# Start-up order and transposes ahead of the values' products in a fused attention and MLP-mixer kernel

## The chip, the cores and the metric

One core of one Trainium2 chip runs the whole program. The metric is device microseconds (us) of one execution, as the median of several runs. The engines have short names below: PE is TensorE (its weight loads are listed as PEld), DVE is VectorE, ACT is ScalarE, POOL is GpSimd, and SP is SyncE, whose queue issues most of the DMAs.

## The reference, cut to what matters

```python
q, k, v: (8, 12, 448, 64) float32      # batch, heads, sequence, head width
def rmsnorm(x, g):
    return x / np.sqrt(np.mean(x * x, axis=-1, keepdims=True) + 1e-06) * g
scores = matmul(rmsnorm(q, g_q), rmsnorm(k, g_k).T) / sqrt(64)
attn = softmax(scores)
x = matmul(attn, v)                     # then (batch, 448, 768), heads side by side
# token and channel mixer; its four weights are float64
u = x + (relu(x.T @ w_tok1) @ w_tok2).T      # 448 -> 256 -> 448
out = u + relu(u @ w_ch1) @ w_ch2            # 768 -> 1536 -> 768
```

## The kernel before, in words

**Work and stages.** The 96 heads are taken as 48 pairs, six pairs for each of the eight batches. The attention of one batch always runs one batch ahead of the mixer of the batch before it. So the program begins with the attention of batch 0 alone ("the first attention"). Beside it, and beside the first mixer, the float64 weights are converted to float32 by bit operations and stored in a form that the later products read back.

**One pair.** `load_qk` (L880) brings queries and keys to SBUF, `squares` (L900) squares them on ACT (L913) into the one buffer `sq` and sums each row on DVE (L917), and `roots` (L926) makes reciprocal roots with ten short DVE operations (L946 to L951). `scale` (L262) multiplies the queries alone by their roots, on POOL (L272). Keys are never scaled: their root goes in as the scale of the exponential on ACT (`exp`, L292). `trans_qk(p, i)` (L274) transposes queries (i = 0) or keys (i = 1) with four PE transposes into a PSUM tile `t_ps` (L282), and ACT brings the tile to the SBUF tile `qkT` with the factor g (L284). `score` (L295) and `score_last` (L308) multiply, and `av` (L397) and `av_last` (L409) form the products with the values; in the first attention each also has a product with a column of ones (L382), which sums the weights. `finish` calls `denominator` (L430), whose four DVE operations begin with the transpose `dt` at L444, which waits for those sums.

**Steps.** `att_step(g)` (L461) is one of four steps s = g mod 4 for two pairs p and p + 1. Each step has `scores()` and then `products()`: s = 0 has the first two score blocks of pair p and the products of the pair before; s = 1 the third block and the first two products; s = 2 the last short blocks of both pairs (L316) and the first block of pair p + 1; s = 3 its two other blocks, then `av_last` of both, a product and `finish(p)`. Behind a step stand items of cost 0: `load_v`; at s = 0 `squares(p + 2)`; at s = 1 `squares(p + 3)`, the roots of both and two `scale`s. At odd s the two `trans_qk` of the next pair come after all these. Below, "step 7" is the step with g = 7.

**Weights.** Chunk i of the weights takes one item, `one(i)` (L230). It issues the load of chunk i + 2, puts bits together for chunk i - 2 on DVE (L209), does the first conversion of chunk i on DVE (L189, L190, L192), the second of chunk i - 1 on ACT (L200, L202), and the last of chunk i - 2 on POOL (L224, and for later weights L163 to L166).

**What sets the order.** The order on PE, DVE, ACT and POOL inside `whole` is that in which the program issues instructions; each engine takes its own strictly in that order. `merge` (L29) mixes the attention's items with the weights' items by their costs. SP's queue is in order too. The four PSUM tiles of `ps_S` are shared by scores and transposes in rotation: a new tile waits until ACT has read the one four tiles earlier. So a pair's `t_ps` at s = 3 takes the tiles of the first score block of the same step, and at s = 1 those of the second block of the step before.

**Start.** The class `Start` runs ahead of the branch on the two gains (`tc.If`). It sets zeros in the five query-and-key buffers on DVE (L850 to L853), loads pairs 0 and 1 (the keys of pair 0 on ACT's queue), makes constants on POOL, and forms squares and roots of pair 0. Then `whole` issues: `load_v(0)`, two weight loads, `scale(0)` on POOL, the change of g at L789, `trans_qk(0, 0)`, `trans_qk(0, 1)`, more loads, and then squares, roots, `swap` and `scale` of pair 1, all ahead of step 0.

Of the kernel before, what the change touches and what calls it, by code (L numbers as in the profile page):

```python
# [46 lines left out]
def whole(ctx, tc, shifted, pre, q, k, v, g_q, g_k, moe_w_tok1, moe_w_tok2, moe_w_ch1, moe_w_ch2, out):  # L47
# [211 lines left out]

        return slice((a ^ p % 2) * D, (a ^ p % 2) * D + D)  # L260

    def scale(p):  # L262

        n = 2 * NS
        qk, rs = st["qk", p], st["rs", p]
        parts = [(R, 0, n, rs[0:R, 0:n].unsqueeze(2))]
        if shifted:
            parts.append((P, n, n - 2, rs[:, n:2 * n - 2].unsqueeze(2)))
            parts.append((P, 2 * n - 2, 2, rs[:, 2 * n - 2:2 * n - 1].unsqueeze(2)))
        for rows, o, m, r in parts:  # L270
            x = qk[0:rows, o * D:(o + m) * D].rearrange("p (r d) -> p r d", d=D)
            nc.gpsimd.tensor_tensor(out=x, in0=x, in1=r.to_broadcast([rows, m, D]), op=ALU.mult)  # L272

    def trans_qk(p, i):  # L274
        qk = st["qk", p]
        if i == 0:
            st["qkT", p] = qkT_pool.tile([P, S + NS * P], F32, name="qkT")
        ps = s_tile("t_ps")
        n = P if i else R
        for c in range(NS):  # L280
            o = (i * NS + c) * P
            nc.tensor.transpose(ps[:, c * n:(c + 1) * n], qk[0:n, o:o + P], ident[0:n, 0:n])  # L282
        to = st["qkT", p][:, S:S + NS * P] if i else st["qkT", p][:, 0:S]
        nc.scalar.mul(to, ps[:, 0:NS * n], g_t[:, i:i + 1])  # L284
        if i == 1:
            st.pop(("qk", p))

    def e_tile():
# [172 lines left out]
    def att_step(g):  # L461


        t, s = divmod(g, 4)
        p = 2 * t
        live = g < NG
        items = []

        def scores():
            if s == 0:  # L470
                score(p, 0)
                score(p, 1)
# [36 lines left out]

        def tiled():  # L510
            if shifted:
                if live:
                    both_shifted()
                return
            if live:
                scores()
            products()

        items.append((3.75 if s in (0, 3) else 2.25, tiled))
        if live and p >= NPAIR and not shifted:  # L520

            parts = {0: [(p, 0)], 1: [(p, 1)], 2: [(p, 2)], 3: [(p + 1, 0), (p + 1, 1), (p + 1, 2)]}[s]
            items += [(0.5, lambda pp=pp, part=part: chunk_sums(pp, part)) for pp, part in parts]
        if live and s % 2 == 1 and p + (s + 1) // 2 < NP:
            items.append((0.0, lambda: load_v(p + (s + 1) // 2)))
        if live and s < 2 and p + 2 + s < NP:
            items.append((0.0, lambda: pre.squares(p + 2 + s, st)))
            if s == 1:
                items.append((0.0, lambda: pre.roots(p + 2, 2, st)))
                items.append((0.0, lambda: swap(p + 3)))  # L530
                items += [(0.0, lambda i=i: scale(p + 2 + i)) for i in range(2)]
        q = p + (s + 1) // 2
        if live and s % 2 == 1 and q < NP:
            items += [(0.4, lambda i=i: trans_qk(q, i)) for i in range(2)]
            if q + 3 < NP:
                items.append((0.0, lambda: pre.load_qk(q + 3, st)))
        return items
# [243 lines left out]
    BEFORE = len(first) + 10  # L781
    then = len(first) + stage_end[4] + 4

    load_v(0)
    weight_load(0)
    weight_load(1)
    scale(0)

    nc.vector.tensor_scalar(g_t[:, 0:1], g_t[:, 0:1], float(D) ** 0.5, None, ALU.mult)  # L789
    trans_qk(0, 0)  # L790
    trans_qk(0, 1)
    pre.load_qk(2, st)
    for i in range(2, 5):
        weight_load(i)
    pre.load_qk(3, st)
    pre.squares(1, st)
    pre.roots(1, 1, st)
    swap(1)
    scale(1)
    per = NPAIR * 2  # L800
    att_items = lambda lo, hi: [it for g in range(lo, hi) for it in att_step(g)]
    for _, fn in merge(att_items(0, AHEAD * per + 1), weight_items(0, BEFORE)):
        fn()
    left = []
    for b in range(B):
# [19 lines left out]
class Start:  # L825


    def __init__(self, ctx, tc, q, k, g_q, g_k, w2):
        self.nc = nc = tc.nc
        self.q, self.k = q, k  # L830
        B, H, S, D = q.shape
        self.NPAIR, self.NS, self.D = H // 2, 4, D
        self.R = S // self.NS
        P = 128
        pool = lambda name, bufs: ctx.enter_context(tc.tile_pool(name=name, bufs=bufs))
        const = pool("start", 1)
        KF = w2.shape[0] // P // 2
        self.hb = const.tile([P, len(HB), KF, S // 2], F32, name="hb")

        n = 2 * self.NS * 2 * D  # L840
        flat = self.hb[:].rearrange("p q f s -> p (q f s)")
        assert flat.shape[-1] >= 2 * n
        self.st = {}
        self.qk_t = [const.tile([P, n], F32, name=f"qk_{i}") for i in range(3)]
        for p in range(2):
            self.st["qk", p] = flat[:, p * n:(p + 1) * n]
        self.v_t = [const.tile([P, (2 * self.NS - 1) * D], F32, name=f"v_{i}") for i in range(2)]

        for qk in [self.st["qk", p] for p in range(2)] + self.qk_t:
            nc.vector.memset(qk[96:P, 0:n // 2], 0.0)  # L850
            o = n - 2 * D
            nc.vector.memset(qk[D:P, o:o + D], 0.0)
            nc.vector.memset(qk[0:D, o + D:o + 2 * D], 0.0)  # L853
        self.load_qk(0, self.st, other=nc.scalar)
        self.load_qk(1, self.st)
        self.g_t = const.tile([P, 2], F32, name="g_t")
        for i, g in enumerate((g_q, g_k)):
            for a in range(2):
                nc.gpsimd.dma_start(
                    out=self.g_t[a * D:(a + 1) * D, i:i + 1], in_=g.rearrange("(p o) -> p o", o=1))  # L860
        self.ident = const.tile([P, P], F32, name="ident")
        make_identity(nc, self.ident[:, :])
        self.one_c = const.tile([P, D], F32, name="one_c")
        nc.gpsimd.memset(self.one_c[:], 1.0)
        self.expo_c = const.tile([P, 1], F32, name="expo_c")
        nc.gpsimd.memset(self.expo_c[:], -896.0 * 2**23)
        self.sq = const.tile([P, 4 * self.NS, D + 1], F32, name="sq")
        nc.gpsimd.memset(self.sq[:, 0:4 * self.NS - 2, D:D + 1], D * 1e-6)
        nc.gpsimd.memset(self.sq[:, 4 * self.NS - 2:4 * self.NS, D:D + 1], D * 0.5e-6)
        self.st["rs", 0] = const.tile([P, 4 * self.NS], F32, name="rs_0")  # L870
        with tc.tile_pool(name="st_0", bufs=1) as self.st_pool:
            self.nt_pool = self.st_pool
            self.squares(0, self.st, halves=((0, 1), (1, 2)))
            self.st.pop(("ms", 0))

    def heads(self, p):
        b, j = divmod(p, self.NPAIR)
# [2 lines left out]
    def load_qk(self, p, st, other=None):  # L880
# [14 lines left out]
                out=k[:, :, a], in_=self.k[b, hs][a][0:nk].rearrange("(p c) d -> p c d", c=NS - 1))  # L895
        for a in range(2):
            o = 4 * NS * D - 2 * D + a * D
            (other or self.nc.sync).dma_start(out=qk[a * D:(a + 1) * D, o:o + D], in_=self.k[b, hs][a][nk:])

    def squares(self, p, st, halves=((0, 2),)):  # L900

# [8 lines left out]
        for lo, hi in halves:  # L910
# [8 lines left out]
            if hi == 2 * n:  # L919

                nc.vector.tensor_tensor(
                    out=ms[:, hi - 2:hi - 1], in0=ms[:, hi - 2:hi - 1], in1=ms[:, hi - 1:hi], op=ALU.add)
            if len(halves) > 1:
# [97 lines left out]
```

## Time and profile before

| | |
|---|---|
| median of 3 runs | 1482.06 us (1481.83 to 1483.47) |
| the profiled execution, whole | 1482.08 us |
| its span, first to last instruction | 1480.3 us |
| PE busy | 1394.3 us (94%), 7048 matmuls |
| DVE busy | 718.4 us (49%) |
| ACT busy | 470.7 us (32%) |
| POOL busy | 475.4 us (32%) |
| first matmul of the scores | starts at 16.49 us |
| last `dt` of the first attention (pair 5) | starts at 100.67 us |

The span runs from the first instruction to the last; 1.8 us of the execution lie around it. In the profile's rows, a number in brackets such as [1.53 <-ACT qkT L284] is the idle time of the engine just before the row, and what ended it. A row "x8" is several instructions that were merged, with the time from the first start to the last end. A matmul in float32 is listed as two records.

### The profile page before, as it was taken

How to read it: one execution, taken by the hardware profiler on the slowest of the kernel's cores; microseconds unless marked ns; L12 is line 12 of the kernel's file. 1: busy time of each engine (PE TensorE's matmuls, PEld its weight loads, DVE VectorE, ACT ScalarE, POOL GpSimd, SP SyncE). 2: the span in 40 equal slices, each digit the busy share in tenths (PEclk: the TensorE clock that was granted, in tenths of full speed). 3: DMA queues.
4: the chain of work that ended last, by engine and by line, in shares of the span. 5: the costliest groups of instructions: out<-in, count | busy, mean ns of one | idle time of the engine just before them, and what ended most of it. 6: DMA issues, size and time to landing. Idle time of an engine off the chain costs nothing.

```text
span 1480.3 us, 19461 instructions
## 1 busy us (share of the span) xinstructions
PE 1394.3 (94%) x7048; PEld 1040.6 (70%) x7048; DVE 718.4 (49%) x1303; ACT 470.7 (32%) x802; POOL 475.4 (32%) x460
## 2 busy tenths in 40 slices
PE   5868767799999999999999999999999999999998
PEld 2324446586777867786777857777677947778998
DVE  7888897833454255433544345432544334331321
ACT  5654343322332234323342233322333223312111
POOL 2455686731233124321333123320332212310321
PEclk9988888899999999999999999999999999999999
DMA  6676677762455524553354625454354624444454
GB/s 151 168 213 183 192 238 216 212 196 84 122 149 144 159 76 138 147 151 112 106 155 127 181 56 153 132 152 130 103 148 124 179 62 128 122 124 134 128 172 135
DMA packets 235212, 214.77 MB, mean 145 GB/s; under 512 B 107140, under 2 KB 191620, under 8 KB 235108
## 3 DMA queue, kind: packets, MB, share of 16 engines
q1 hardware_dynamic: 211746, 202.20, 47.5%
q10 hardware_dynamic: 23234, 11.24, 2.7%
q8 instruction: 58, 0.95, 0.3%
q14 instruction: 46, 0.38, 0.1%
q0 software_dynamic: 128, 0.00, 0.0%
HBM read 185.86 MB, written 27.53 MB: 144 GB/s over the span
## 4 chain that ended last, share of the span: by engine, by line
PE 80%; POOL 1%; DMA 1%; DVE 1%; issue 1%; ACT 0%; SPq 0%; ACTq 0%; POOLq 0%
PE m_ps L704 26%; PE m_ps L647 23%; PE s_ps L302 7%; PE o_ps L403 6%; PE m_ps L566 5%; PE m_ps L574 4%; PE t_ps L545 3%; PE d_ps L382 2%; PE t_ps L282 2%; PE s_ps L316 1%; PE o_ps L415 1%; DMA unit<-ws 0%; POOL stage L224 0%; DMA ws<-stage 0%; POOL stage L164 0%
## 5 line engine op out<-in xcount | busy, mean ns | idle before, releaser
L704 PE MATMUL m_ps<-hb,unit 128*128 128x224 f32 x2016 | 402.7, 355 | 8.8 <-DMA unit<-ws 8.8
L704 PEld LDWEIGHTS m_ps<-hb,unit 128*128 128x128 f32 x2016 | 376.0, 191 | 28.7 <-issue 17.1
L292 ACT ACTIVATE e<-s_ps,rs 128x448 f32<-128x448 f32 x336 | 187.4, 633 | 214.2 <-PE s_ps L302 142.3
L647 PE MATMUL m_ps<-tu,unit 128*128 128x224 f32 x1152 | 238.9, 360 | 0.0
L647 PEld LDWEIGHTS m_ps<-tu,unit 128*128 128x128 f32 x1152 | 218.5, 194 | 15.7 <-PE o_ps L403 4.9
L647 PE MATMUL m_ps<-uT,unit 128*128 128x224 f32 x864 | 178.3, 359 | 9.3 <-DVE hb L652 6.1
L647 PEld LDWEIGHTS m_ps<-uT,unit 128*128 128x128 f32 x864 | 162.7, 192 | 28.8 <-issue 17.1
L302 PE MATMUL s_ps<-qkT 64*128 64x448 f32 x576 | 139.6, 588 | 5.9 <-ACT qkT L284 5.2
L272 POOL TENSOR_TENSOR qk<-qk,rs 112x512 f32<-112x512 f32 x46 | 51.1, 1132 | 265.5 <-DVE rs L951 189.2
L713 POOL TENSOR_TENSOR uT<-uT,r 128x448 f32<-128x448 f32 (+1 forms) x64 | 57.0, 901 | 245.6 <-DVE r L713 160.1
L403 PE MATMUL o_ps<-e,v 128*64 128x448 f32 x576 | 132.1, 562 | 0.0
L363 POOL TENSOR_TENSOR es<-e 128x896 f32<-128x896 f32 x42 | 88.3, 2102 | 63.3 <-ACT sq L913 47.6
L713 DVE TENSOR_TENSOR uT<-uT,m_ps 128x448 f32<-128x448 f32 (+1 forms) x80 | 38.9, 502 | 130.0 <-PE m_ps L704 127.8
L652 DVE TENSOR_TENSOR r<-m_ps,r 128x448 f32<-128x448 f32 x72 | 44.8, 622 | 117.6 <-POOL r L652 67.1
L566 PE MATMUL m_ps<-x,w_sb 112*128 112x384 f32 x256 | 92.4, 508 | 9.5 <-DVE x L551 9.5
L444 DVE STREAM_TRANSPOSE dt<-d_ps 128x448 f32<-128x448 f32 x42 | 27.3, 650 | 152.3 <-PE d_ps L382 152.3
L284 ACT ACTIVATE qkT<-t_ps,g_t 128x448 f32<-128x448 f32 x96 | 60.6, 657 | 127.3 <-PE t_ps L282 127.2
L369 DVE TENSOR_TENSOR es<-es,e 128x896 f32<-128x896 f32 x42 | 48.0, 1143 | 106.6 <-ACT e L292 75.8
L302 PEld LDWEIGHTS s_ps<-qkT 64*128 64x128 f32 x576 | 49.7, 191 | 68.3 <-issue 54.6
L403 PEld LDWEIGHTS o_ps<-e,v 128*64 128x64 f32 x576 | 33.0, 137 | 87.8 <-issue 85.0
L653 ACT ACTIVATE hb<-hb 128x448 f32<-128x448 f32 x72 | 41.7, 579 | 156.2 <-DVE hb L652 132.6
L574 PE MATMUL m_ps<-w_sb,h 128*128 128x448 f32 x192 | 80.0, 562 | 6.6 <-DVE uT L579 6.6
(85 smaller groups left out, 1478.2 us busy)
## 6 DMA issues: line engine op xcount, KB each, us to landing
unit<-ws SPq DMA_DIRECT2D x336, 384.0 KB, 3.2
raw<-in_moe_w_ch_dram SPq DMA_DIRECT2D x72, 256.0 KB, 3.3
ws<-stage SPq DMA_DIRECT2D x36, 448.0 KB, 3.3
out_dram<-y ACTq DMA_DIRECT2D x48, 224.0 KB, 3.3
qk<-in_q_dram SPq DMA_DIRECT2D x92, 112.0 KB, 3.2
v<-in_v_dram SPq DMA_DIRECT2D x48, 192.0 KB, 2.8
qk<-in_k_dram SPq DMA_DIRECT2D x92, 96.0 KB, 3.2
raw<-in_moe_w_tok_dram SPq DMA_DIRECT2D x4, 448.0 KB, 5.1
```

What stands on the lines that cost most here:

```text
L272: nc.gpsimd.tensor_tensor(out=x, in0=x, in1=r.to_broadcast([rows, m, D]), op=ALU.mult)
L284: nc.scalar.mul(to, ps[:, 0:NS * n], g_t[:, i:i + 1])
L292: nc.scalar.activation(out=out, in_=ps[:, 0:S], func=AF.Exp, scale=st["rs", p][:, r:r + 1])
L302: nc.tensor.matmul(out=pss[a][:, 0:S], lhsT=qkT[a * D:(a + 1) * D, o:o + P], rhs=qkT[a * D:(a + 1) * D, 0:S], start=True, stop=True)
L363: nc.gpsimd.tensor_tensor(out=es[:], in0=st["e", p, 0][:], in1=st["e", p, 1][:], op=ALU.add)
L369: nc.vector.tensor_tensor(out=es[:], in0=es[:], in1=st["e", p, 2][:], op=ALU.add)
L403: nc.tensor.matmul(out=o[a * D:(a + 1) * D, 0:S], lhsT=vt[:, c:c + D], rhs=e[:, a, :], start=start, stop=stop)
L566: nc.tensor.matmul(out=ps[:, 0:HC], lhsT=w1_sb[0:R, c, jc * P:(jc + 1) * P], rhs=st["x", h][0:R, c, :], start=(c == 0), stop=(c == NS - 1))
L574: nc.tensor.matmul(out=ps[:, 0:S], lhsT=st["h1", jc][:, cc * P:(cc + 1) * P], rhs=w2_sb[:, jc].rearrange("p c r -> p (c r)"), start=(jc == ...
L647: nc.tensor.matmul(out=ps[:, j * HS:(j + 1) * HS], lhsT=w[:, t, j, :], rhs=m, start=(t == 0), stop=(t == KC - 1))
L704: nc.tensor.matmul(out=ps[:, j * HS:(j + 1) * HS], lhsT=st["w"](j, t), rhs=hb[:, HB[what], t, :], start=(t == 0), stop=(t == KF - 1))
L713: add = lambda e, o, x, y: e.tensor_tensor(out=o, in0=x, in1=y, op=ALU.add)
```

## The change

Three things are changed.

First, `Start` lets ACT run a `Square` of one column at once, so that its table of functions is loaded there. Pair 0's buffer gets only its two small zero blocks; the three later buffers are zeroed by POOL. The short last rows of pair 0's keys are loaded on SP's queue instead of ACT's. Only the queries of pair 0 are squared in `Start`.

Second, in `whole` the order for pair 0 becomes: g, transposes of the keys, `scale(0)` on DVE instead of POOL, squares and roots of the keys, transposes of the queries. Squares, roots, `swap` and `scale` of pair 1 (`second_pair`) move from ahead of step 0 to behind the items of step 0, and the last of these items is `squares(2)`.

Third, at odd steps below 11 the two `trans_qk` of the next pair are issued inside the step, between its scores and its products, instead of after the step's other items.

```diff
-    def scale(p):
+    def scale(p, eng=nc.gpsimd):
...
-            nc.gpsimd.tensor_tensor(out=x, in0=x, in1=r.to_broadcast([rows, m, D]), op=ALU.mult)
+            eng.tensor_tensor(out=x, in0=x, in1=r.to_broadcast([rows, m, D]), op=ALU.mult)
...
             if live:
                 scores()
+            if inside:
+                for i in range(2):
+                    trans_qk(q, i)
             products()
...
+        q = p + (s + 1) // 2
+        turned = live and s % 2 == 1 and q < NP
+        inside = turned and g < 2 * NPAIR - 1 and not shifted
...
-        q = p + (s + 1) // 2
-        if live and s % 2 == 1 and q < NP:
-            items += [(0.4, lambda i=i: trans_qk(q, i)) for i in range(2)]
+        if turned:
+            if not inside:
+                items += [(0.4, lambda i=i: trans_qk(q, i)) for i in range(2)]
...
+    nc.vector.tensor_scalar(g_t[:, 0:1], g_t[:, 0:1], float(D) ** 0.5, None, ALU.mult)
+    if not shifted:
+        trans_qk(0, 1)
+        scale(0, nc.vector)
+        pre.squares(0, st, halves=((1, 2),))
+        trans_qk(0, 0)
...
     load_v(0)
     weight_load(0)
     weight_load(1)
-    scale(0)
-
-    nc.vector.tensor_scalar(g_t[:, 0:1], g_t[:, 0:1], float(D) ** 0.5, None, ALU.mult)
-    trans_qk(0, 0)
-    trans_qk(0, 1)
     pre.load_qk(2, st)
     for i in range(2, 5):
         weight_load(i)
     pre.load_qk(3, st)
-    pre.squares(1, st)
-    pre.roots(1, 1, st)
-    swap(1)
-    scale(1)
+
+    def second_pair():
+        pre.squares(1, st)
+        pre.roots(1, 1, st)
+        swap(1)
+        scale(1)
+
-    for _, fn in merge(att_items(0, AHEAD * per + 1), weight_items(0, BEFORE)):
+    for _, fn in merge(
+            att_items(0, 1) + [(0.0, second_pair)] + att_items(1, AHEAD * per + 1), weight_items(0, BEFORE)):
         fn()
...
-        for qk in [self.st["qk", p] for p in range(2)] + self.qk_t:
-            nc.vector.memset(qk[96:P, 0:n // 2], 0.0)
-            o = n - 2 * D
-            nc.vector.memset(qk[D:P, o:o + D], 0.0)
-            nc.vector.memset(qk[0:D, o + D:o + 2 * D], 0.0)
+        warm = const.tile([P, 1], F32, name="warm")
+        nc.vector.memset(warm[:], 1.0)
+        nc.scalar.activation(out=warm[:], in_=warm[:], func=AF.Square)
+        self.zeros(nc.vector, self.st["qk", 0])
         self.load_qk(0, self.st, other=nc.scalar)
+        for i, qk in enumerate([self.st["qk", 1]] + self.qk_t):
+            eng = nc.gpsimd if i else nc.vector
+            self.zeros(eng, qk)
+            eng.memset(qk[96:P, 0:n // 2], 0.0)
         self.load_qk(1, self.st)
...
-            self.squares(0, self.st, halves=((0, 1), (1, 2)))
+            self.squares(0, self.st, halves=((0, 1),))
...
+    def zeros(self, eng, qk):
+
+        D, P = self.D, 128
+        o = qk.shape[-1] - 2 * D
+        eng.memset(qk[D:P, o:o + D], 0.0)
+        eng.memset(qk[0:D, o + D:o + 2 * D], 0.0)
...
-            (other or self.nc.sync).dma_start(out=qk[a * D:(a + 1) * D, o:o + D], in_=self.k[b, hs][a][nk:])
+            self.nc.sync.dma_start(out=qk[a * D:(a + 1) * D, o:o + D], in_=self.k[b, hs][a][nk:])
```

The branch for large gains (`shifted`), which these inputs do not take, is changed in its own way and left out here.

More of the change, by code (lines that the diff above doesn't have):

```diff
@@ L271, in scale @@
             x = qk[0:rows, o * D:(o + m) * D].rearrange("p (r d) -> p r d", d=D)
-            nc.gpsimd.tensor_tensor(out=x, in0=x, in1=r.to_broadcast([rows, m, D]), op=ALU.mult)
+            eng.tensor_tensor(out=x, in0=x, in1=r.to_broadcast([rows, m, D]), op=ALU.mult)
     def trans_qk(p, i):
         qk = st["qk", p]
-        if i == 0:
+        if ("qkT", p) not in st:
             st["qkT", p] = qkT_pool.tile([P, S + NS * P], F32, name="qkT")
@@ L284, in trans_qk @@
         nc.scalar.mul(to, ps[:, 0:NS * n], g_t[:, i:i + 1])
-        if i == 1:
+        if p and i == 1 or p == 0 and i == 0:
             st.pop(("qk", p))
@@ L782, in whole @@
     then = len(first) + stage_end[4] + 4
+    nc.vector.tensor_scalar(g_t[:, 0:1], g_t[:, 0:1], float(D) ** 0.5, None, ALU.mult)
[4 more added lines that the diff above has]
+        trans_qk(0, 0)
+    else:
+        pre.squares(0, st, halves=((1, 2),))
+        scale(0)
+        trans_qk(0, 1)
+        trans_qk(0, 0)
+    st.pop(("ms", 0))
     load_v(0)
@@ L922, in squares @@
                     out=ms[:, hi - 2:hi - 1], in0=ms[:, hi - 2:hi - 1], in1=ms[:, hi - 1:hi], op=ALU.add)
-            if len(halves) > 1:
+            if hi - lo == n:
                 self.roots(p, 1, st, lo, hi, rows)
```

## The prediction

> **What bounds the kernel now.** I read the busy time by stage first, then the timeline of the first 62 us, then the waits of the first attention.
>
> ```profile
> core 0: us, PE busy (x) PEld busy (x) DVE busy (x) ACT busy (x) POOL busy (x), PEclk, DMA share, GB/s
> 0.00:16.00 16.00, 1.83 (x8) 1.46 (x8) 9.81 (x43) 3.21 (x5) 4.24 (x15) 1.00 0.67 150
> 16.00:31.00 15.00, 12.32 (x54) 5.00 (x56) 11.99 (x36) 11.12 (x18) 1.24 (x2) 1.00 0.72 182
> 31.00:62.00 31.00, 26.99 (x153) 10.14 (x150) 29.09 (x49) 20.85 (x37) 14.28 (x14) 0.98 0.54 151
> ...
> 107.00:340.00 233.00, 186.42 (x848) 136.14 (x849) 174.85 (x249) 83.40 (x142) 144.00 (x152) 0.88 0.69 207
> 340.00:1480.00 1140.00, 1130.77 (x5826) 874.33 (x5823) 457.47 (x871) 326.35 (x561) 288.61 (x251) 1.00 0.46 130
> ```
>
> From 340 us on PE is busy 1130.8 of 1140 us; the change touches nothing there. It touches the first 107 us. There DVE sets the pace once it runs: 29.1 of 31 us from 31 to 62.
>
> ```profile
> 6.51 1.28 ACT L913 ACT_TABLE_LOAD   x1 [6.51 <-DMA hb<-in_k_dram]
> ...
> 11.95 1.08 POOL L272 TENSOR_TENSOR hb<-hb,rs 112x512 f32<-112x512 f32 x1 [7.73 <-DVE nt L949]
> ...
> 13.13 1.83 PE L282 MATMUL t_ps<-ident,hb 112*128 112x112 f32 x8 [13.13 <-DVE rs L951]
> ...
> 16.33 1.05 ACT L913 ACTIVATE sq<-hb 128x1024 f32<-128x1024 f32 x1
> ...
> 16.49 4.33 PE L302 MATMUL s_ps<-qkT 64*128 64x448 f32 x12 [1.53 <-ACT qkT L284]
> ...
> 20.93 1.06 ACT L913 ACTIVATE sq<-qk 128x1024 f32<-128x1024 f32 x1
> ...
> 21.07 1.04 POOL L272 TENSOR_TENSOR hb<-hb,rs 112x512 f32<-112x512 f32 x1 [8.04 <-ACT e L292]
> ...
> 23.91 1.04 PE L282 MATMUL t_ps<-ident,hb 112*128 112x112 f32 x8
> ...
> 28.11 0.97 PE L316 MATMUL s_ps<-qkT 64*64 64x448 f32 x4 [1.60 <-ACT qkT L284]
> ```
>
> The start is one chain: queries land, the table is loaded, square, sum, roots, `scale`, transposes, evictions, scores at 16.49. Beside it pair 1 is squared at 16.33 (its input is named hb, pair 2's qk), so `scale(1)` starts at 21.07, while PE works through steps 0 and 1 up to 23.91.
>
> ```profile
> ACT e_t L200 <- DVE e_t L192: 17.6, 7, 5.9
> ...
> DVE dt L444 <- PE m_ps L382: 7.3, 3, 4.0
> ...
> PE s_ps L316 <- ACT qkT L284: 5.8, 2, 4.2
> ...
> PE s_ps L302 <- ACT qkT L284: 5.2, 4, 2.0
> ```
>
> These waits are of the first 110 us. PE waits 11.0 us for evictions, but the longest waits lie in a loop: a weight's ACT step waits for DVE, the exponentials queue behind it, PE waits for those, and in the end DVE waits for PE's sums.
>
> [...] eight transposes take 1.83 us at 13.13 and 1.04 us at 23.91; after the idle stretch before 61.16 they take 1.83 us again, and PE is back at full rate only at about 67.8. [...]
>
> **The change part by part.**
>
> *Start, down to the first scores.* The queries' first DMA goes out at 1.89 because it waits for a memset of its rows; without it, it can go at 1.17, and without pair 1's keys ahead of it. It landed at 6.42; I take 5.6. The table load is then over. Square 0.63, sum 0.69 and ten root steps of 0.20 (9.75 to 11.73, no longer mixed with the keys' steps) give roots at 9.1. DVE takes 0.65 us for its branch (14.26 to 14.91), g 0.2, `scale` 0.69: 10.7. Transposes of the queries 0.85 (cold, half of 1.83), eviction 0.65: first scores at 12.3 instead of 16.49, so **4.2 us earlier**. Landing as before and the price of POOL give 13.4. The keys' square, sum and roots then lie on DVE until 13.6, ahead of the first exponentials at 14.2. POOL's nine memsets delay the g loads (four issues, 2.2 us) by some 2 us, to about 9, hidden behind the queries' chain.
>
> *Pair 1 moved.* By the costs in `merge` the order becomes chunk 0, step 0, `squares(2)`, pair 1, chunk 1, step 1. So ACT squares **pair 2 before pair 1**. Pair 2's last piece was issued at 14.28 and landed near 17.9 (the piece ahead: 13.61 to 17.59). SP now has two more issues of 0.6 us ahead of `whole`, less two waits that fall away: 0.5 us later, 18.4. Then, with `sq` a single buffer: square of pair 2 to 19.5, its sum to 20.75, only then square of pair 1 to 21.85, sum 1.25 to 23.15, add 0.2, roots 2.06 to 25.4, `scale(1)` 1.08 on POOL to 26.6. In the kernel before it ended at 22.1.
>
> *Transposes ahead in step 1.* They need `scale(1)`, and the products of step 1 are now queued behind them on PE. PE has done its scores by 16 and idles 10 us to 26.7, where nothing covers. Cold: transposes 1.83 to 28.5; products 3.2 us warm (20.75 to 23.9), I take 4.3 (two groups at 1.33 to 1.53 instead of 0.92 to 0.97, as at 67.08 and 83.74) to 32.8; the two short blocks and the next full one 2.75 to 35.6. Before, that block ended at 29.96. The waits of 0.59 and 1.60 us for exponentials and evictions are gone, but PE is **5.6 us behind**. Beyond: squares of pair 3 follow the evictions at 29, so DVE idles 27.3 to 30 and reaches its next conversion 3 us late.
>
> *Step 3.* Products of step 2 (1.65) and scores (1.7) end at 38.95. The transposes of pair 2 need the PSUM tiles of this step's first score block, thus two exponentials, to 39.5; they take 1.04; then `av_last` with its ones, 1.65: sums ready at 42.2. Before, 34.98. DVE would come to this `dt` at 38.3 and waits, with all conversions behind it. It was at 35.27: DVE is 6.9 us behind. The wait of 0.86 us at 38.54 is saved: PE is 5.3 behind at step 4. DVE's work to the next `dt` (43.55, where it had waited 0.38) is solid, so 6.55 remain, up to chunk 6's L192 and the exponentials of step 7.
>
> *Step 7.* Before, its products ran while ACT stood behind chunk 6, and only the transposes waited, to 61.16. Now products wait too: transposes from 67.7 to 69.5, `av_last` and ones cold 3.2 to 72.7, where DVE wanted `dt` at 69.0. Products, scores and products of step 8 (1.8, 1.75, 3.2) give the next `dt` at 79.4 instead of 70.71: **8.7 behind**. Both ends: warm at once, 7; cold throughout, 10.
>
> *Steps 9 to 12.* Evictions of pair 5 precede the square of pair 7, which removes the 4.21 us of PE idle before 80.85; on DVE that saves only its wait of 0.98. At step 11, still with its transposes last, the second eviction no longer stands behind a weight's 1.17 us (92.15 to 93.32). 8.7 - 0.98 - 1.17 = 6.6 behind at the last `dt`.
>
> *After that.* The orders and merges from step 12 on are the old ones. DVE is busy 175 of 233 us from 107 to 340, POOL 144 and PE 186; none is full, they wait for each other in turn, so all start 6.6 late and stay so. I cost absorption at nothing; the bound is the whole 6.6. The profiled time is 1482.08, 0.02 above the median: 1482.1 + 6.6 = **1488.7 us**.
>
> **The rivals.** *Faster: the lead is kept.* If `scale(1)` were ready when step 1's scores end, PE would keep its 4.2 us and most of the 11 us of eviction waits would go from PE; DVE holds the rest back, so 1482.1 - 4.2 = 1478. What decides is whether `scale(1)` is done before about 22, as before. Against it stand the two squares in one buffer and the landing at 18. *Unchanged: absorbed.* The idle quarter of DVE and PE between 107 and 340 takes up the delay; 1482 to 1485. For it: neither engine is full. Against it: everything there, loads included, is chained to what starts late. *Worse: the PSUM wait.* The order in odd steps puts PE cold at steps 3 and 7 for longer than I take, and nothing is given back at 9 to 11: 1482.1 + 10 to 12 = 1493. That the change does nothing is excluded, as every engine's order changes.
>
> **How the numbers follow.** The likeliest case has 0.66, with its own range 1484.8 to 1492.5: pair 2's landing +-1, cold rate of PE in step 1 -1.1 to +1, step 7 -1.7 to +1.3, some absorbed. Absorbed 0.14, faster 0.10, worse 0.10. The range 1483.0 to 1492.5 leaves out faster, part of absorbed and most of worse. A measurement of this kernel can tell about 0.2% from no change (1479.1 to 1485.0), which gives faster 0.10, same 0.14, slower 0.76.
>
> **What would show it.** Right: table load near 1 us, first scores near 12.3; the square of qk before the second square of hb; PE idle from 16 to about 26.7 ahead of the transposes of hb; the block after the short ones ending near 35.6; first `dt` near 42; PE idle of about 8 us before step 7's transposes; last `dt` near 107. Wrong: `scale(1)` done by 22, or a first `dt` within 2 us of 35.3. If the last `dt` is late but 340 us is not, absorption was right.

## The result, and the profile after

The changed kernel takes 1490.41 us (median of 4 runs, 1487.68 to 1491.23), against 1482.09 us for the kernel before (4 runs beside them, 1481.83 to 1483.47). The ratio is 1.0051, 95% interval 1.0034 to 1.0068: slower by 8.3 us, where 6.6 us was forecast. The profiled execution took 1489.63 us with a span of 1487.8, so the two traces differ by 7.5 us in their spans.

Three views answer to those of before. First the busy time by stage; the last stage is shifted with the work.

```profile
core 0: us, PE busy (x) PEld busy (x) DVE busy (x) ACT busy (x) POOL busy (x), PEclk, DMA share, GB/s
0.00:16.00 16.00, 5.78 (x18) 3.34 (x20) 8.19 (x37) 5.40 (x9) 5.53 (x23) 1.00 0.61 145
16.00:31.00 15.00, 5.22 (x22) 2.37 (x20) 8.48 (x22) 7.45 (x11) 1.04 (x1) 0.66 0.78 187
...
347.00:1487.00 1140.00, 1130.87 (x5826) 874.42 (x5824) 457.74 (x871) 326.36 (x561) 287.93 (x251) 1.00 0.46 130
```

Up to 16 us PE does more than before (5.78 us against 1.83). From 16 to 31 us it does less than half (5.22 against 12.32), and all other engines do less too; only the DMAs are busier (0.78 against 0.72). The lead of the start is lost there, and much more. From 347 us on nothing has changed: PE was busy 1130.77 of 1140 us before, 1130.87 now.

The timeline shows where.

```profile
1.31 1.28 ACT L870 ACT_TABLE_LOAD   x1 [1.31 <-PEq L1034]
...
9.84 0.69 DVE L272 TENSOR_TENSOR hb<-hb,rs 112x512 f32<-112x512 f32 x1
...
12.32 4.71 PE L302 MATMUL s_ps<-qkT 64*128 64x448 f32 x12 [0.72 <-ACT qkT L284]
...
18.52 1.06 ACT L942 ACTIVATE sq<-qk 128x1024 f32<-128x1024 f32 x1 [1.65 <-DMA qk<-in_k_dram]
...
20.88 1.06 ACT L942 ACTIVATE sq<-hb 128x1024 f32<-128x1024 f32 x1 [1.30 <-DVE ms L946]
...
25.71 1.04 POOL L272 TENSOR_TENSOR hb<-hb,rs 112x512 f32<-112x512 f32 x1 [19.15 <-DMA v<-in_v_dram]
26.81 1.86 PE L282 MATMUL t_ps<-ident,hb 112*128 112x112 f32 x8 [9.78 <-POOL hb L272]
...
33.49 1.02 PE L302 MATMUL s_ps<-qkT 64*128 64x448 f32 x4
...
40.72 0.65 DVE L444 STREAM_TRANSPOSE dt<-m_ps 128x448 f32<-128x448 f32 x1 [2.04 <-PE m_ps L382]
```

Here hb is again pair 1 and qk pair 2 (the `hb` of 9.84 is pair 0's queries). Pair 2 is squared first, when its load has landed (18.52); pair 1 has been in SBUF for long and is squared after it (20.88). `scale(1)`, the POOL row, ends at 26.75 instead of 22.11. (Its bracket names a load of values, which `scale` does not read; the last root step of pair 1 on DVE ends at 25.48.) PE stands idle for 9.78 us, in front of the transposes, with step 1's products queued behind them.

Then the waits of the first attention, from 0 to 115 us (total, times, longest).

```profile
PE t_ps L282 <- issue: 10.2, 2, 6.7
PE t_ps L282 <- POOL hb L272: 9.8, 1, 9.8
DVE dt L444 <- PE m_ps L382: 9.3, 4, 3.7
```

PE's waits for evictions (`s_ps` behind `qkT`, 11.0 us before) are nearly gone: L302 has 1.5 us of them in the whole run, L316 none up to 115 us. In their place stand one wait of 9.8 us for `scale(1)` and two of 10.2 us together ahead of transposes, at steps 7 and 11 (before: one of 3.15 us, at step 7). The longest of these is at step 7, where exponentials (65.50) stand behind a weight's step on ACT and PE now holds back its products as well. Before, PE had done these products by 58.02; the two fences show the kernel before, then the changed one:

```profile
61.16 1.83 PE L282 MATMUL t_ps<-ident,qk 112*128 112x112 f32 x8 [3.15 <-issue]
```

```profile
64.32 0.72 ACT L200 ACTIVATE e_t<-e_t,expo_c 128x512 uint32<-128x512 uint32 x1 [5.91 <-DVE e_t L192]
...
65.50 2.19 ACT L292 ACTIVATE e<-s_ps,rs 128x448 f32<-128x448 f32 x4
...
66.22 1.83 PE L282 MATMUL t_ps<-ident,qk 112*128 112x112 f32 x8 [6.74 <-issue]
...
71.28 0.65 DVE L444 STREAM_TRANSPOSE dt<-m_ps 128x448 f32<-128x448 f32 x1 [3.69 <-PE m_ps L382]
```

The same landmarks in both traces (us from the start of the span) give the delay along the way:

| | before | after | delay |
|---|---|---|---|
| first scores start | 16.49 | 12.32 | -4.17 |
| `scale(1)` ends | 22.11 | 26.75 | +4.64 |
| first full score block of step 2 ends | 30.03 | 34.52 | +4.49 |
| first `dt` | 35.27 | 40.72 | +5.45 |
| second `dt` | 43.55 | 48.56 | +5.01 |
| third `dt` (step 7) | 62.47 | 71.28 | +8.81 |
| fourth | 70.71 | 77.83 | +7.12 |
| last of the first attention | 100.67 | 105.13 | +4.46 |
| first of the second attention | 143.17 | 149.09 | +5.92 |
| a `dt` near 300 us | 298.42 | 305.48 | +7.06 |
| a `dt` near 374 us | 374.10 | 381.18 | +7.08 |
| span | 1480.29 | 1487.83 | +7.54 |

### The profile page after: what moved, and what is told of

It reads as the page before. It is cut to its first block, busy times and chain, and to the rows that moved or that the text cites. A ratio compares the mean times of both kernels' runs of the same rounds, so it can differ in the third digit from the quotient of the medians.

```text
span 1487.8 us, 19459 instructions
## 1 busy us (share of the span) xinstructions
PE 1395.8 (94%) x7048; PEld 1043.3 (70%) x7048; DVE 716.8 (48%) x1295; ACT 470.5 (32%) x803; POOL 476.1 (32%) x468
## 4 chain that ended last, share of the span: by engine, by line
PE 79%; POOL 1%; DMA 1%; DVE 1%; issue 1%; ACT 0%; SPq 0%; ACTq 0%; POOLq 0%
PE m_ps L711 26%; PE m_ps L654 23%; PE s_ps L302 6%; PE o_ps L403 6%; PE m_ps L573 5%; PE m_ps L581 4%; PE t_ps L552 3%; PE d_ps L382 2%; PE t_ps L282 2%; PE o_ps L415 1%; PE s_ps L316 1%; DMA unit<-ws 1%; POOL stage L224 0%; DMA ws<-stage 0%; POOL stage L164 0%
## 5 line engine op out<-in xcount | busy, mean ns | idle before, releaser
L302 PE MATMUL s_ps<-qkT 64*128 64x448 f32 x576 | 140.6, 585 | 2.8 <-ACT qkT L284 1.5
L573 PE MATMUL m_ps<-x,w_sb 112*128 112x384 f32 x256 | 93.4, 512 | 10.0 <-DVE x L558 10.0
L284 ACT ACTIVATE qkT<-t_ps,g_t 128x448 f32<-128x448 f32 (+1 forms) x96 | 60.7, 659 | 127.1 <-PE t_ps L282 125.5
L302 PEld LDWEIGHTS s_ps<-qkT 64*128 64x128 f32 x576 | 50.8, 190 | 66.9 <-issue 53.2
```

Of the source, the lines that this page charges most:

```text
L302: nc.tensor.matmul(out=pss[a][:, 0:S], lhsT=qkT[a * D:(a + 1) * D, o:o + P], rhs=qkT[a * D:(a + 1) * D, 0:S], start=True, stop=True)
L573: nc.tensor.matmul(out=ps[:, 0:HC], lhsT=w1_sb[0:R, c, jc * P:(jc + 1) * P], rhs=st["x", h][0:R, c, :], start=(c == 0), stop=(c == NS - 1))
```

## The experiments

My theory was the prediction's: pair 1 is made late by the order of its squares, and the transposes put ahead of the products make PE wait for it, and again at step 7. The rivals were that the start itself costs the time, or that one of the two moves does it alone. "Before" below is always the kernel before on the same chip; times in us from ratios are (ratio - 1) x 1483.

| kernel | ratio to before | 95% interval | first `dt` | third `dt` | last `dt` |
|---|---|---|---|---|---|
| before | 1 | | 35.27 | 62.47 | 100.67 |
| after, run again | 1.0055 | 1.0043 to 1.0067 | 41.79 | 72.32 | 106.83 |
| pair1_first | 1.0025 | 1.0015 to 1.0035 | 37.44 | 67.97 | 102.54 |
| no_inside | 1.0014 | 1.0007 to 1.0020 | 38.36 | 65.74 | 103.52 |
| start_only | 1.0011 | 1.0004 to 1.0018 | 37.67 | 65.04 | 104.22 |
| inside_only | 1.0009 | 1.0003 to 1.0016 | 36.51 | 66.99 | 101.67 |
| start_s1 | 1.0002 | 0.9994 to 1.0010 | 36.23 | 63.62 | 101.94 |
| near_s1 | 1.0007 | 0.9999 to 1.0015 | 35.18 | 63.66 | 99.63 |
| near_loads | 0.9994 | 0.9986 to 1.0002 | 34.31 | 61.66 | 97.14 |
| step1_only | 1.0037 | 1.0022 to 1.0051 | 40.02 | 67.39 | 104.77 |
| not_step1 | 1.0062 | 1.0049 to 1.0074 | 41.13 | 71.32 | 107.83 |
| not_step1b | 1.0033 | 1.0023 to 1.0044 | 37.83 | 68.06 | 101.73 |
| late_weights | 0.9976 | 0.9967 to 0.9985 | 34.91 | 58.58 | 95.28 |

The `dt` columns are of one profiled execution each.

**Pair 1 ahead of pair 2's squares (pair1_first).** The transposes stay ahead of the products.

```diff
-            att_items(0, 1) + [(0.0, second_pair)] + att_items(1, AHEAD * per + 1), weight_items(0, BEFORE)):
+            att_items(0, 1)[:1] + [(0.0, second_pair)] + att_items(0, 1)[1:] + att_items(1, AHEAD * per + 1), weight_items(0, BEFORE)):
```

> The changed kernel with one edit: pair 1's squares, roots and scale are issued straight behind step 0, ahead of squares(2), instead of behind it. Theory (the wait of step 1 is the main loss): pair 1 is squared at 17 instead of 20.9, its scale ends at about 22.6 instead of 26.8, PE's idle time ahead of the transposes of pair 1 falls from 9.8 to about 5.5 us, the first dt comes at about 37 instead of 40.7, and the whole is some 4 us shorter than the changed kernel: about 1486. Rival (the transposes ahead at steps 3 and 7 are the main loss): no more than 1 us shorter, about 1489.5, since DVE is caught by them again. Rival (the lead of the start is kept once pair 1 is ready in time): about 1478.

In the timeline of this kernel the two longest waits of PE in the first attention are:

```profile
22.61 1.86 PE L282 MATMUL t_ps<-ident,hb 112*128 112x112 f32 x8 [5.42 <-POOL hb L272]
...
62.91 1.83 PE L282 MATMUL t_ps<-ident,qk 112*128 112x112 f32 x8 [6.73 <-issue]
```

`scale(1)` ends at 22.56, the first wait is 4.4 us shorter and the run 4 us shorter than after. The wait of step 7 is unchanged: it does not come from pair 1.

**The old place of the transposes (no_inside).**

```diff
-        inside = turned and g < 2 * NPAIR - 1 and not shifted
+        inside = False
```

> The changed kernel with one edit: all transposes stand behind the products and items again, as before the change; the new start and the place of pair 1 behind squares(2) stay. Theory: the products of step 1 run at 17 to 20.5 in the idle time, the transposes of pair 1 still wait to 26.7, the second step's scores end near 31.5 (29.96 in the kernel before, 34.4 in the changed one), the first dt is 1 to 2 us later than the 35.27 of the kernel before, and step 7 costs nothing: about 1483.5. Rival (the move of pair 1 alone is the loss, whatever stands behind the transposes): about 1488 to 1490.

Slower than before by 2.1 us, where 1.4 was expected, with the first `dt` 3.1 us late (1 to 2 expected). The late `scale(1)` now stops PE only after step 1's products, but it still does:

```profile
27.21 1.86 PE L282 MATMUL t_ps<-ident,hb 112*128 112x112 f32 x8 [7.31 <-POOL hb L272]
```

**The new start alone (start_only).** Both edits together: pair 1 first, transposes in the old place.

> The changed kernel with both edits: pair 1 ahead of squares(2), and all transposes behind the products and items. What is left is the new start: table at once, keys' transposes first, scale of pair 0 on DVE. Theory: the scores start at 12.3, but scale(1) ends at about 22.6, no earlier than before (22.1), so the lead of 4.2 us dies there; first dt within 1 us of 35.27, whole time 1481 to 1482.5. Rival (the lead is kept): first dt near 31, whole time about 1478.

This missed: slower by 1.6 us. `scale(1)` is early, first scores come at 12.24, and still the first `dt` is 2.4 us late. From the kernel's timeline, PE's rows and then ACT's:

```profile
22.63 1.04 PE L282 MATMUL t_ps<-ident,hb 112*128 112x112 f32 x8 [2.39 <-POOL hb L272]
23.60 1.74 PE L316 MATMUL s_ps<-qkT 64*64 64x448 f32 x4
27.78 1.76 PE L316 MATMUL s_ps<-qkT 64*64 64x448 f32 x4 [2.44 <-ACT qkT L284]
```

```profile
25.57 1.06 ACT L942 ACTIVATE sq<-qk 128x1024 f32<-128x1024 f32 x1 [3.22 <-DMA v<-in_v_dram]
26.53 1.20 ACT L284 ACTIVATE qkT<-t_ps,g_t 128x448 f32<-128x448 f32 x2
```

PE comes early and finds the next thing not there: 2.39 us for `scale(1)`, then 2.44 us for an eviction that stands on ACT behind the square of pair 3, and that square waits for DMA: pair 3's loads were issued by SP from 18.20 to 22.46, the values' load that the bracket names just after them. After the first gap a group of short scores takes 1.74 us, which took 0.97 us in the kernel before. So the lead turns into idle time of PE, and behind it PE has half clock: from 18 to 61 us the granted clock is 0.88 in this run, 1.00 in the kernel before. This speaks against the rival "lead kept" as well: `scale(1)` at 22.57 was not enough for it.

**The transposes ahead on the old start (inside_only).** The kernel before, with the `inside` lines of the diff alone.

> The kernel before with one edit: at odd steps below 11 the transposes stand between the scores and the products; start and place of pair 1 are the old ones. Theory: the transposes of pair 1 wait only from 20.9 to about 22.2, step 2 ends 0.8 us earlier, the first dt is 0 to 1 us later than 35.27, step 7 costs 2 us at the fourth dt (PE idle some 6 us ahead of its transposes), and steps 9 to 11 give 2 to 2.5 us back: 1481.5 to 1483. Rival (transposes ahead cost by themselves): 1485 or more. Rival (they gain, as the evictions' waits go): 1478 or less.

Slower by 1.3 us, a little more than expected (-0.6 to +0.9 against 1482.1). At step 7 PE waits 6.73 us ahead of the transposes (3.15 us in the kernel before), and the third `dt` is 4.5 us late; all but 1.0 us is given back by the last `dt`. On the new start four kernels form a square: neither move (start_only) +1.6, late pair 1 alone (no_inside) +2.1, transposes ahead alone (pair1_first) +3.7, both (the changed kernel) +7.6 to +8.2. The moves add 0.5 and 2.1 us when single and some 6 us together. The surplus of 3.4 to 4.0 us is larger than its uncertainty, some 2.7 us by an estimate from the four intervals. Late pair 1 is cheap as long as the products of step 1 stand ahead of its transposes and cover part of the wait.

**The changed kernel again (after_again).** No edit.

> The changed kernel once more, beside the three below on one chip and with more rounds. Expected: 7 to 8 us over the kernel before (ratio 1.005); a second trace tells which part of the delay behind the first attention (4.5 us at its last dt, 7.1 us at 325 us in the first trace) is the kernel's own and which is PE's clock: if it is the kernel's own, the same growth appears again.

+8.2 us; the result repeats. So does the growth behind the first attention: the delay is 6.16 us at the last `dt` and 9.05 us near 300 us. By what was expected, that speaks for the kernel itself; the next section comes back to it.

**Ahead of the products only at s = 1 (start_s1).** As start_only, with

```diff
-        inside = False
+        inside = turned and g < 2 * NPAIR - 1 and not shifted and s == 1
```

> The changed kernel with pair 1 ahead of squares(2), and transposes between scores and products only at steps 1, 5 and 9; at steps 3 and 7 they stand behind the products as before the change. Theory (at steps 3 and 7 the products stand behind a wait for exponentials): against pair1_first, the first dt is 1 us earlier (36.4), PE's idle time ahead of step 7's transposes is 3.2 instead of 6.7 us, the fourth dt 2 us earlier (73), and the whole 1 to 2 us shorter: 2 us over the kernel before. Rival (the loss that pair1_first keeps comes from step 1 alone): no shorter than pair1_first, 3.5 us over before.

1.0002, better than the 2 us over that were expected: not distinguishable from before, while start_only's interval lies above the kernel before. Against pair1_first this run is 3.4 us faster, and its wait at step 7 is the old one:

```profile
62.33 1.83 PE L282 MATMUL t_ps<-ident,qk 112*128 112x112 f32 x8 [3.43 <-issue]
```

So on this start the order costs 3.4 us at s = 3 (steps 3 and 7), where the tiles of the transposes wait for exponentials of the same step, and nothing that could be measured at s = 1 (1.3 us less than start_only, which is within the two intervals).

**The transposes straight behind the step (near_s1).** As start_only, but at s = 1 the two `trans_qk` come after the products, but ahead of the squares and evictions of the step's other items.

```diff
+        near = turned and g < 2 * NPAIR - 1 and not shifted and s == 1
         items.append((3.75 if s in (0, 3) else 2.25, tiled))
+        if near:
+            items += [(0.4, lambda i=i: trans_qk(q, i)) for i in range(2)]
```

> The changed kernel with pair 1 ahead of squares(2), and at steps 1, 5 and 9 the transposes straight behind the products, ahead of load_v and squares(3) or its like; at steps 3, 7, 11 as before the change. Nothing stands behind a wait that did not before, and evictions of pair 1 no longer stand behind the square of pair 3, which waits for its load until 25.5. Theory: transposes of pair 1 at 22.6, scores of step 2 from about 25 instead of 27.8 (start_only), first dt set by DVE at 34.5 to 35.3, the idle 4 us of PE at step 10 gone, so 0 to 2 us below the kernel before. Rival (PE's cold clock after the idle stretch at 20 eats it): 1 to 2 us above, as start_only.

PE keeps the lead here (the full block of step 2 ends at 26.47, 30.03 before), but the first `dt` stays at 35.18: DVE sets it. The last `dt` is 1.0 us early, and after 107 us that is lost again. The time is not distinguishable from before; the gain that was hoped for is not there, and the rival's 1 us over is not excluded.

**The same with pair 2's and 3's loads earlier in SP's queue (near_loads).**

```diff
     weight_load(0)
-    weight_load(1)
     pre.load_qk(2, st)
+    weight_load(1)
+    pre.load_qk(3, st)
     for i in range(2, 5):
         weight_load(i)
-    pre.load_qk(3, st)
```

> near_s1 with one more edit: on SP's queue the loads of pair 2 stand ahead of the second weight load, and those of pair 3 ahead of the third to fifth. If the arrival of pairs 2 and 3 is what holds the lead (their squares waited until 18.5 and 25.5), the square of pair 3 starts near 23, DVE reaches the next conversion at about 28.5 instead of 30.7, the first dt comes near 33, and the whole is 2 to 4 us below the kernel before. Rival (DVE's own work from 15 to 31 sets it, whatever arrives): as near_s1.

Now the square of pair 3 starts at 24.96 without a wait, behind both evictions, and the first `dt` comes at 34.31. The last `dt` is 3.5 us earlier than before (near_s1: 1.0), so the loads had held part of the lead back. Of this 2.4 us are lost again by 298 us in the profiled execution, and the ratio, 0.9994, does not exclude no change: less than the 2 to 4 us expected.

**Ahead at step 1 alone (step1_only).** From the changed kernel:

```diff
-        inside = turned and g < 2 * NPAIR - 1 and not shifted
+        inside = turned and g == 1 and not shifted
```

> The changed kernel with transposes between scores and products at step 1 alone; at all later odd steps they stand behind the products and items as before the change. Pair 1 stays behind squares(2). Theory (the wait of step 1, with products behind it, is the biggest single loss): PE idle for nearly 10 us to 26.8, the second step's scores end near 34.5, first dt near 39.5, and the whole 5 to 6 us over the kernel before (ratio 1.0035 to 1.004), so 3 us over no_inside. Rival (steps 3 and 7 make the loss): as no_inside, 2 us over before.

+5.5 us, as expected. Against no_inside the one edit costs 3.4 us, and what differs in the trace is the wait of step 1 with the products behind it (PE idle 9.62 us ahead of the transposes; in no_inside it is 7.31, and the products are done by then).

**Everywhere but at step 1 (not_step1, not_step1b).**

```diff
-        inside = turned and g < 2 * NPAIR - 1 and not shifted
+        inside = turned and 1 < g < 2 * NPAIR - 1 and not shifted
```

> The changed kernel with transposes between scores and products at steps 3, 5, 7 and 9, and at step 1 behind the products and items as before the change. Pair 1 stays behind squares(2). Theory: products of step 1 run at 17 to 20.5, second step's scores end near 33.3 as in no_inside, step 3 puts the first dt near 39.5, step 7 idles 6.7 us, steps 9 to 11 give some back: 3 to 4 us over the kernel before (1.002 to 1.0027). Rival (step 1 is nothing special, the loss is the order of the pairs and steps 3 and 7): 7 us over, as the changed kernel.

This missed altogether: +9.2 us, worse than the change itself. But the edit did more than was meant. The two transposes of step 1 are items of cost 0.4 again, and `merge` now put chunk 2 of the weights ahead of step 2 and chunk 3 ahead of step 3:

```profile
36.50 0.67 ACT L200 ACTIVATE e_t<-e_t,expo_c 128x448 uint32<-128x448 uint32 x1 [3.65 <-DVE e_t L192]
...
38.30 1.13 PE L282 MATMUL t_ps<-ident,qk 112*128 112x112 f32 x8 [3.29 <-issue]
```

ACT stands 3.65 us before a weight's step, step 3's exponentials stand behind it, and the transposes wait for those with the products behind them. So a second version gives these two items a cost of 0 at step 1, which leaves the mix with the weights as it was in the changed kernel:

```diff
-                items += [(0.4, lambda i=i: trans_qk(q, i)) for i in range(2)]
+                items += [(0.4 if g > 1 else 0.0, lambda i=i: trans_qk(q, i)) for i in range(2)]
```

> not_step1 with the two transposes of pair 1 at cost 0 in the merge instead of 0.4 each, so that every chunk of weights keeps its place of the changed kernel; in not_step1 the cost had put chunk 3 ahead of step 3, and step 3's exponentials and transposes stood 3.3 us behind it. Theory (step 1's wait with products behind it costs by itself): PE has no idle 3.3 us ahead of step 3's transposes, first dt at 38.5 to 39.5, and the whole 4 to 6 us over the kernel before (1.003 to 1.004). Rival (step 1's wait is covered elsewhere, the rest is the loss): 7 us or more over before (1.005), as the changed kernel.

+4.9 us and a first `dt` at 37.83. So step 1's order is worth about 3 us of the change (8.2 - 4.9, and 3.4 from step1_only), that of steps 3 to 9 together about 2 to 3 (4.9 - 2.1). Each of these differences is uncertain by 2 to 2.5 us, by an estimate from the intervals. And the place of two weight chunks costs 4.3 us here (9.2 - 4.9), about as much as the transposes' move alone (3.7).

**The weights one place later (late_weights).** near_loads' order of the loads and pair1_first's order of pairs, the transposes behind the products inside the step, and, behind the first weights' item, an empty one that only delays the others:

```diff
+            products()
             if inside:
                 for i in range(2):
                     trans_qk(q, i)
-            products()
...
+    early = weight_items(0, BEFORE)
+    early.insert(1, (0.3, lambda: None))
```

> A version drawn from the runs so far: new start, pair 1 ahead of squares(2), loads of pairs 2 and 3 ahead of weight loads as in near_loads, transposes at odd steps below 11 straight behind the step's products, and the weights' items from the second on 0.3 later in the merge, so that steps 1 and 7 go ahead of the chunk whose ACT part waits for DVE. Theory: the exponentials of step 7 no longer stand behind chunk 6, the half-clock stretch of PE near 60 us and its idle time of 3.7 us go, dt at steps 7 and 8 come 3 us earlier than in near_loads, and the whole is 4 to 6 us below the kernel before. Rival (DVE's work sets the pace, so what PE gains there is waited for later): as near_loads, 1 us below.

0.9976 (0.9967 to 0.9985): 3.6 us faster than before, a little under the 4 to 6 expected, and the only version whose interval lies below the kernel before. At step 7, in its timeline:

```profile
52.95 2.21 ACT L292 ACTIVATE e<-s_ps,rs 128x448 f32<-128x448 f32 x4 [0.28 <-PE s_ps L302]
```

```profile
56.92 1.04 PE L282 MATMUL t_ps<-ident,qk 112*128 112x112 f32 x8
```

The exponentials no longer stand behind a waiting weight step, the transposes run at full rate without a wait before them (1.04 us; 1.83 in the kernel before, after 3.15 us idle), and the third `dt` comes 3.9 us early. It combines four edits and was not taken apart further; the wait at step 7 is gone, but which share each edit has is not shown.

## Why the prediction was right, point by point

**Start.** Right: scores at 12.32 (12.3 forecast). The table load ran at 1.31 for 1.28 us, and `scale` on DVE took 0.69 us at 9.84, as forecast; the trace of before, where it runs on POOL in 1.08 us, did not show that figure. Queries were squared at 5.61. One small term was off: the transposes of the queries took 1.01 us where 0.85 was taken (and half of 1.83 is 0.92); `scale`, done at 10.53 instead of 10.7, made up for it.

**Pair 1 moved.** Right in mechanism and size: squares at 18.52 and 20.88 (18.4 and 20.8), end of `scale(1)` 26.75 (26.6). pair1_first shows that it counts: undoing this alone takes 4 us off.

**Step 1.** The idle time was right (9.78, forecast 10), the products cold a little dear (3.98 us from 28.60 to 32.58, 4.3 forecast; the granted clock is 0.50 to 30.3 us). What was over-sized is the term of 2.75 us for the two short blocks and the next full one: with both pairs' evictions done, the eight records of the two short blocks ran in 0.98 us, as long as four took before (0.97 at 28.11), and the full block took 1.02, 1.94 us in all (1.93 in the second trace). It ends at 34.52 instead of 35.6, so 4.5 behind instead of 5.6. step1_only and not_step1b confirm the part played by the order: some 3 us.

**Step 3.** First `dt` at 40.72 (5.45 late), not 42.2 (6.9). 1.1 us of that comes from step 1; the wait of the transposes for two exponentials, which I put at 0.55 us (38.95 to 39.5), was not there: they start at 37.89 without a gap.

**Step 7.** Right: PE idle 6.74 us (8 forecast), the transposes' 1.83 us cold (the granted clock is 0.50 from 61.0 to 71.3 us), DVE waiting 3.69 us for `dt` (72.7 - 69.0 = 3.7 forecast). `dt` comes at 71.28 instead of 72.7, and the next one is 7.12 behind instead of 8.7. What step 7 adds was right: 2.1 us from the second to the fourth `dt` (5.01 to 7.12), forecast 2.15; the rest is what steps 1 and 3 had too much. inside_only and start_s1 show that the step 7 term belongs to the order, not to pair 1.

**Steps 9 to 12.** The sign was right: 7.12 behind shrank to 4.46 at the last `dt`, by 2.66 us where 2.15 was taken. PE's 4.21 us of idle time at step 10 are gone, as forecast. A new wait of 3.49 us ahead of step 11's transposes, whose exponentials stand behind a weight's step that waits 5.99 us for DVE, was not in the forecast. So at 105 us the delay was 2.1 us less than forecast (4.46, not 6.6).

**After that.** The step that failed in size: "all start 6.6 late and stay so". In the profiled execution the delay did not stay: it grew from 4.46 us at 105 us to 7.06 us at 305 us, and stood at 7.08 at 381 us. So the forecast of +6.6 for this execution (measured +7.5) is two errors which nearly cancel, and that much of the agreement is luck. The second trace (after_again) is nearer to the forecast up to the last `dt` (first `dt` at 41.79, third at 72.32, the last 6.16 behind), because the products of step 1 took 4.8 us in it; but there, too, the delay grows, to 9.05 us near 300 us. 1.46 us of the growth can be located in one group, the mixer's first product at tok1, in the kernel before (L566) and after (L573):

```profile
128.70 7.12 PE L566 MATMUL m_ps<-x,w_sb 112*128 112x384 f32 x16 [4.01 <-DVE x L551]
```

```profile
133.17 8.57 PE L573 MATMUL m_ps<-x,w_sb 112*128 112x384 f32 x16 [4.53 <-DVE x L558]
```

It is the same work after a similar wait, 1.45 us longer, and in the clock record 6.8 us at half rate lie there (before 3.4). All fourteen traces of this study fall in two kinds by this row. In five of the changed kernels (after, after_again, near_s1, near_loads, not_step1b) the group takes 8.41 to 8.66 us, and from the last `dt` to the one near 300 us they lose 2.3 to 2.9 us against the kernel before. In the other eight, and before, it takes 6.99 to 7.12 us, and the eight change by -0.5 to +0.4 us. Where in the span the work lies does not decide: not_step1b and start_s1 have their last `dt` at 101.73 and 101.94 and fall on different sides.

What goes with it is how the work lies against the clock. In the clock records the granted clock changes only at points 3.41 us apart (in before and after it is 1.00 or 0.50, and up to 1470 us the stretches at 0.50 are 3.41, 6.83 or 10.24 us long), and a stretch at half rate ended only behind an interval in which PE paused for less than 0.47 us (the counts are in the last section). In the five traces PE is still idle for 0.27 to 0.78 us of the interval with which this half rate begins, and the half rate goes on for another 3.41 us; in the other nine it is idle for at most 0.23 us there, and the full rate comes back. That accounts for 1.45 us. Where the other 1.1 us of the growth come from is not shown.

Run back to the start, the first of these points lies anywhere from 0.3 to 3.2 us behind the first instruction in the fourteen traces, so how the work lies against them is not set by the program alone. But this does not clear the change of the growth. Both traces of the changed kernel are of the long kind, and the four kernels with the transposes in their old place from step 3 on (before, no_inside, start_only, step1_only) have no idle time at all in that interval. How often each kernel falls on either side, one or two traces of it cannot tell; so what share of the growth belongs to the change stays open. Executions of near_s1 do spread by that much (14 runs, 1481.70 to 1486.53, the profiled one the slowest). Over all runs the changed kernel is 7.6 to 8.2 us slower, more than the 4.46 and 6.16 us of its last `dt` in the two profiled executions.

**The rivals.** "Absorbed" is false: the delay stands to the end. (Smaller delays did shrink: pair1_first was 1.87 us behind at the last `dt` and 0.78 at 374 us.) "Faster, the lead is kept" was not met: `scale(1)` came at 26.75. With `scale(1)` at 22.57 (start_only), close to the rival's condition of about 22, the kernel was still slower by 1.6 us: PE then waited for an eviction behind the square of pair 3 (2.44 us) and ran at half rate (1.76 us for short scores that take 0.97 in the kernel before). "Worse", 1493 us, was not reached; what it names, a longer wait at step 7, was the 6.74 us already in the sum.

## What to carry to other kernels

Moving work forward on an engine that takes its queue in order moves forward its wait as well (here PE's 9.78 us, with step 1's products behind it): ask which finished work now stands behind it, and when its input will be there, before asking what it saves. Two moves can cost more than the sum of what each costs alone (here some 6 us against 2.6) when one takes away the cover that the other relied on, so test them in pairs. And a lead at the start is worth only what the next load, eviction and square can take up.

## What was not expected of the hardware

In the kernel before, PE's idle time of 3.15 us ahead of step 7's transposes was followed by half rate (the granted clock is 0.50 from 61.0 to 67.8 us, 1.00 on both sides). Shorter gaps were enough: in start_only a gap of 2.39 us was followed, one group of transposes later, by short scores at 1.74 us (0.97 at 28.11 in the kernel before, at a granted clock of 1.00), in late_weights a gap of 2.16 us by 2.69 us for both short blocks (1.90 in near_s1 after a gap of 1.91 us, where the full block kept its 1.02 us). So one wait more can cost PE twice.

Nor is it the length of a gap alone. Near 1200 us, where nothing was changed, every one of the fourteen traces has a gap of 2.38 to 2.40 us in PE's work with the same group behind it. In ten the clock stayed full. In after_again, start_s1, near_s1 and late_weights a stretch of 3.41 us at half rate began 1.1 to 1.4 us after the gap, and the delay jumped by 1.6 us (9.35 to 10.92 in after_again). The row behind the gap in the kernel before, then in after_again:

```profile
1206.06 1.77 PE L574 MATMUL m_ps<-w_sb,h 128*128 128x448 f32 x4 [2.39 <-DVE uT L579]
```

```profile
1215.39 2.17 PE L581 MATMUL m_ps<-w_sb,h 128*128 128x448 f32 x4 [2.38 <-DVE uT L586]
```

In the fourteen clock records every change lies at the end of one of a row of intervals of 3.41 us, and PE's idle time in each of these can be counted. Of 5638 intervals at full rate, all 155 with 1.95 us of idle time or more were followed by half rate, none of the 5446 with less than 1.44 us, and 4 of the 37 between. Of 329 intervals at half rate, all 157 with 0.23 us of idle time or less were followed by full rate, and none of the 169 with 0.47 us or more. Near 1200 us the four traces have 2.02 to 2.28 us of the gap in one interval, the other ten at most 1.85. So in these traces a gap of 2 us that fell into one interval lost the full rate, and only an interval with less than 0.47 us of idle time brought it back.

From 18 to 61 us the change lowered PE's granted clock from 1.00 to 0.88 (the third column from the end), while PE did less work there (36.97 us busy in the kernel before, whose row stands first, and 32.15 after):

```profile
18.00:61.00 43.00, 36.97 (x198) 13.42 (x194) 39.53 (x83) 29.59 (x50) 14.60 (x14) 1.00 0.56 152
```

```profile
18.00:61.00 43.00, 32.15 (x164) 12.81 (x164) 34.05 (x75) 26.22 (x43) 10.50 (x9) 0.88 0.54 140
```

Executions of one kernel spread about as far as the differences looked for: the kernel before had 136 runs beside these experiments, from 1480.8 to 1487.3 us. Two traces of the changed kernel differ by 1.07 us at the first `dt` (40.72 and 41.79) and by 3.74 us in their spans, of which 1.6 us are the stretch near 1200 us. Landmarks of single traces show where time goes; only the ratios of many runs say how much.
